# Local and pooled attention with a gated feed-forward: k and v in shared buffers, sums and half a softmax on other engines, an order chosen by replays

## Chip, cores and metric

The kernel runs on one core of one Trainium2 chip. The metric is device time of one execution in microseconds (us), lower is better; it is the median of several timed runs. Engines are named as the profile names them: PE (TensorE), PEld (its weight loads), DVE (VectorE), ACT (ScalarE), POOL (GpSimd), SP (the queue that issues most transfers).

## What is computed

Inputs are q, k and v of shape 8 x 8 x 576 x 64 (batch, heads, sequence, head dimension) and four weights. Cut to what matters:

```python
q_d, k_d, v_d = (mean of 4 neighbouring tokens of q, k, v)      # 144 rows
out_up  = repeat(softmax(q_d @ k_d.T / 8) @ v_d, 4)             # pooled attention
mask    = abs(i - j) < 4                                        # band: 7 keys for a query
out_loc = softmax(where(mask, q @ k.T / 8, -1e9)) @ v           # local attention
x = (out_up + out_loc) as 4608 tokens x 512
return ((x @ w1) * (x @ w2)) @ w3 @ w_out                       # 512 -> 1024 -> 1024 -> 512
```

All is float32; the large products run as three matmuls on high and low parts.

## The kernel before

Sequence and batch are cut into 24 units of 192 tokens (3 for each batch); two units make a chunk of 384 tokens, the piece that the feed-forward (`moe`) takes, so there are 12 chunks.

**Weights.** `fold` multiplies w3 and w_out into one matrix (tiles accw, then wphl); `gate_weights` makes high and low parts of w1 and w2. Each of the 40 pieces comes over DMA as 64-bit words (tile raw) and is turned into float32 by ACT or POOL (L293, L295), DVE (L298, L302) and ACT (L285).

**Pooled attention.** For each batch four `pair` calls make scores (s_ps), softmax (pexp: maximum on DVE L459, four exponentials on ACT L468, which also sum, scaling on POOL L477), transposes on PE (L484) and copies (pt). The values give oup. For batches 2 to 7 the sums over four tokens are made by accumulating DMAs that POOL issues (qks L410, vs L411).

**Local attention has two forms.** Batches 0 and 1 (units 0 to 5) are done in groups on PE (`group_unit`, `group_scores`, `group_values`): two quads a unit, 12 in all, each with scores of 128 x 432 elements in tile se. The mask is added (L627), then DVE takes the maximum (L636), subtracts it (L637), ACT takes the exponential (L638), DVE sums (L639), adds 1e-9, inverts (L640, L641) and scales (L642). PE transposes (te_ps) and multiplies by v.

Batches 2 to 7 (18 units) are done in `unit` on 128 partitions with 12 tokens each. For each of the seven offsets in the band, DVE multiplies q by the shifted k (tile pr, L727), and the product is summed over the head dimension by DVE (L740) or, for two offsets, by ACT in pieces with an accumulator (L737). After a softmax over seven values (tile s_t, L747 to L763), v times each weight is made by DVE (L794) or, for two offsets, by ACT (L786). Six additions sum the seven products into xl: the first and third by DVE (L804), the other four by an accumulating DMA from the tile pv into xl, which POOL issues (L802). DVE then turns the tile (L808), adds oup (L815), and the high and low parts go to chunk tiles xh and xl (ACT L821, DVE L822). The one buffer of k_t is loaded anew when the last product with it is done; v_t has two, pv three.

**Feed-forward.** For each chunk and each of eight f, PE makes two products (pab, 12 matmuls of 384 columns each), ACT copies the first (L870), DVE multiplies (tile a, L872), ACT and DVE make high and low parts (gh L877, gl L879), and PE accumulates into three banks (acc, 9 matmuls of 512 columns). Two sets of chunk tiles alternate.

**Order.** Each step is a task of a plan with an engine, a cost and what it depends on. `Plan.order` simulates the plan forwards and backwards 16 times with the costs as given and keeps the order with the least end. That order is fixed: each engine runs its own list from top to bottom, and a waiting instruction holds up all that stand behind it on its engine. PSUM has three banks for attention (ps), two for pab and three for acc.

Of the kernel before, what the change touches and what calls it, by code (L numbers as in the profile page):

```python
# [8 lines left out]
F32 = mybir.dt.float32  # L9
# [37 lines left out]
BUFS = dict(pr=3, pv=3, xl=2, xt=1, q=2, k=1, v=2, w3=5, early_raw=4, early_wx=2, late_raw=2, late_wx=2, a=2,  # L47
# [3 lines left out]
SHARE = dict(qk_pool=(), qk_act=(2, 4), av_act=(3, 5), dma_add=(2, 4, 5, 6))  # L51
# [3 lines left out]
ROUNDS = 16  # L55
# [24 lines left out]
class Plan:  # L80
# [29 lines left out]
    def run(self, prio, slack, back=False):  # L110
# [25 lines left out]
        while best:  # L136
            e = min(best, key=lambda e: best[e][0])
            s, i = best[e]
            t = tasks[i]
            x = s + t.cost  # L140
            free[e] = x
            again = {e}
            if t.late and back:
                dma = max(dma, s + 0.8) + t.late
                x = dma + 1.3 + t.cost
            elif t.late:
                dma = max(dma, x + 1.3) + t.late
                x = dma + 0.8
            start[i], end[i] = s, x
            order.append(i)  # L150
            ready[e].remove(i)
            for j in suc[i]:
                can[j] = max(can[j], x + (0.0 if e == tasks[j].eng == "PE" else LATENCY))
                left[j] -= 1
                if not left[j]:
                    ready[tasks[j].eng].append(j)
                    again.add(tasks[j].eng)
            for j in () if back else self.then[i]:
                can[j] = max(can[j], s)
                left[j] -= 1  # L160
                if not left[j]:
                    ready[tasks[j].eng].append(j)
                    again.add(tasks[j].eng)
            for e in sorted(again):
                if e in free:
                    choose(e)
        return max(end), start, end, order

    def order(self):

# [5 lines left out]
        now = self.run([-x for x in far], 0.05)  # L176
        best = now
        for _ in range(ROUNDS):
            back = self.run([-x for x in now[2]], 0.05, back=True)
            now = min((self.run([-x for x in back[2]], z) for z in SLACKS), key=lambda r: r[0])  # L180
            best = min(best, now, key=lambda r: r[0])
        self.best = best
        return [self.tasks[i] for i in best[3]]
# [26 lines left out]
def tile_attention_moe(ctx: ExitStack, tc: tile.TileContext, q, kw, vw, qk4, v4, w1, w2, w3, wout, edge, out):  # L210
# [234 lines left out]
    def pair(b, Q, P, lq, hq, hpt):  # L445
# [33 lines left out]
        for par in range(2):  # L479
            def flip(par=par):  # L480
# [4 lines left out]
            fl, bank = add("PE", 4 * 0.062, flip, [no], take=[R["ps"]], uses=[hp])  # L485

# [70 lines left out]
    def group_unit(n):  # L557
# [21 lines left out]
        def rest():  # L579
            hpt = None  # L580
            pts = []
            for qd, (U, hs, no) in enumerate(quads):
                for par in range(2):
                    def flip(par=par, U=U):
# [3 lines left out]
                    fl, bank = add("PE", NG * 0.062, flip, [no], take=[R["ps"]], uses=[hs])  # L588

# [9 lines left out]
                    pep.append(fl)  # L599
# [4 lines left out]
    def group_scores(b, j, qd, starts):  # L604
# [32 lines left out]
        t = add("DVE", dve_us(n2), lambda: nc.vector.tensor_tensor(out=p3(), in0=p3(), in1=wide_(U["mx"]), op=ALU.subtract), [t], uses=[hs])  # L637
        t = add("ACT", act_us(n2), lambda: nc.scalar.activation(out=U["p"], in_=U["p"], func=AF.Exp, scale=1.0 / D ** 0.5), [t], uses=[hs])  # L638
        t = add("DVE", dve_us(n2), lambda: nc.vector.tensor_reduce(out=U["sm"], in_=p3(), op=ALU.add, axis=AX.X), [t], uses=[hs])  # L639
        t = add("DVE", 0.16, lambda: nc.vector.tensor_scalar_add(U["sm"], U["sm"], 1e-9), [t], uses=[hs])  # L640
        t = add("DVE", 0.15, lambda: nc.vector.reciprocal(U["sm"], U["sm"]), [t], uses=[hs])  # L641
        no = add("DVE", dve_us(n2), lambda: nc.vector.tensor_tensor(out=p3(), in0=p3(), in1=wide_(U["sm"]), op=ALU.mult), [t], uses=[hs])  # L642
# [55 lines left out]
    def unit(n):  # L698
# [9 lines left out]
        def load_k():  # L708
            T["k"] = pools["dvp"].tile([128, nk], F32, name="k_t", bufs=BUFS["k"])
            nc.sync.dma_start(out=T["k"], in_=kw[b, :, j * nq:j * nq + nk])  # L710

        def load_v():
            T["v"] = pools["dvp"].tile([128, nk], F32, name="v_t", bufs=BUFS["v"])
            nc.sync.dma_start(out=T["v"], in_=vw[b, :, j * nq:j * nq + nk])
        lq, hq = add("SP", 0.5, load_q, take=[R["q"]], late=dma_us(128 * nq * 4))
        lk, hk = add("SP", 0.5, load_k, take=[R["k"]], late=dma_us(128 * nk * 4))
        lv, hv = add("SP", 0.5, load_v, take=[R["v"]], late=dma_us(128 * nk * 4))
# [55 lines left out]
        for i, o in enumerate(order):  # L773
# [26 lines left out]
            else:  # L800
                if i in share["dma_add"]:
                    t = add("Pool", 1.04, lambda o=o: nc.gpsimd.dma_start(out=T["x"], in_=T["pv", o], accum_op=ALU.add), [t, tm], uses=[hx, h], late=dma_us(128 * nq * 4, True))  # L802
                else:
# [23 lines left out]
    def moe(c):  # L827
# [56 lines left out]
        for i in range(3):  # L884
# [5 lines left out]
            def store(i=i):  # L890
                if c * CT // S in PB:
                    nc.sync.dma_start(out=out[c * CT + i * 128:c * CT + i * 128 + 128], in_=T["o", i])
                    return
                b, t = divmod(c * 2 * UT + i * 8, BT)
                if t + 8 <= BT:
                    nc.sync.dma_start(out=out_v[b, t:t + 8], in_=T["o", i])
                else:
                    r = BT - t
                    nc.sync.dma_start(out=out_v[b, t:], in_=T["o", i][:r * NB])
                    nc.sync.dma_start(out=out_v[b + 1, :8 - r], in_=T["o", i][r * NB:])  # L900
# [118 lines left out]
```

## Time and profile before

| | us |
|---|---|
| median of 3 timed runs | 819.2 |
| lowest and highest | 814.92, 820.14 |
| profiled execution | 811.43 |
| its span (first to last instruction) | 809.6 |
| PE, DVE, ACT, POOL busy in the span | 763.1, 645.4, 525.1, 200.3 |

The granted clock of PE was 0.987 over the span. Times in the trace count from the start of the span. The windows view gives each engine's busy time in a stretch; a busy time is the union of an engine's instructions. A row of a group gives count, busy time, mean length of one, and after the bar the idle time of the engine just before them with what ended it. A row of the waits view gives the sum of a wait, how often it came, and the longest. DVE starts an instruction some 0.08 us before the one ahead of it ends, so the starts of two long ones lie closer than one length.

### The profile page before, as it was taken

The numbers are of one execution on the slowest core, as the hardware profiler recorded it, in microseconds if no ns is written. First come the engines' busy times: TensorE is split into PE (matmuls) and PEld (weight loads), VectorE is DVE, ScalarE is ACT, GpSimd is POOL, SyncE is SP. The second block draws the span as 40 slices with busy tenths as digits, with TensorE's granted clock in tenths as the row PEclk, the third lists the DMA queues.
The fourth block names the chain that finished last, engine by engine and source line by source line (L and its number), as shares of the span: only waits on it lengthen the run. The fifth ranks groups of instructions, "written<-read, shape, count | busy, mean of one in ns | idle before, by whom it ended". The sixth has DMA issues, their size and how long they took to land.

```text
span 809.6 us, 15110 instructions
## 1 busy us (share of the span) xinstructions
PE 763.1 (94%) x5256; PEld 657.2 (81%) x5256; DVE 645.4 (80%) x1121; ACT 525.1 (65%) x2040; POOL 200.3 (25%) x211
## 2 busy tenths in 40 slices
PE   4899888999999999999999999999997999999995
PEld 1344467898999899998998999798997988999994
DVE  5889997967899998998999989799886898853111
ACT  4676656445877878867877697587783788742211
POOL 5321666300221323321312221222221221110000
PEclk9999999999999999999999999999998999999998
DMA  8975654813389759947858659855576853351101
GB/s 289 303 243 186 192 138 148 163 43 128 108 196 213 152 125 221 191 116 182 179 128 216 146 101 225 182 119 126 137 169 154 185 116 81 72 104 20 40 1 39
DMA packets 44067, 118.98 MB, mean 147 GB/s; under 512 B 5320, under 2 KB 11464, under 8 KB 43992
## 3 DMA queue, kind: packets, MB, share of 16 engines
q0 software_dynamic: 15264, 46.02, 32.5%
q1 hardware_dynamic: 28728, 72.01, 27.4%
q8 instruction: 41, 0.67, 0.3%
q14 instruction: 34, 0.28, 0.1%
HBM read 80.26 MB, written 9.44 MB: 111 GB/s over the span
## 4 chain that ended last, share of the span: by engine, by line
PE 59%; DVE 15%; DMA 14%; ACT 6%; issue 4%; POOL 0%; SPq 0%; DVEq 0%; ACTq 0%; POOLq 0%
PE pab L253 12%; PE pab L255 11%; PE pab L254 11%; PE acc L253 6%; PE acc L255 6%; PE acc L254 6%; DMA k_t<-in_kw_dram 4%; DMA xl<-pv 4%; DMA out_dram<-o_sb 3%; DVE pr L727 2%; DMA raw<-in_w_dram 2%; PE s_ps L456 2%; DVE wx L302 1%; ACT pexp L468 1%; DMA raw<-in_wout_dram 1%
## 5 line engine op out<-in xcount | busy, mean ns | idle before, releaser
L786 ACT ACTIVATE pv<-v_t,s_t 128x64 f32<-128x64 f32 x432 | 114.1, 343 | 28.3 <-DMA xl<-pv 16.1
L727 DVE TENSOR_TENSOR pr<-q_t,k_t 128x768 f32<-128x768 f32 x126 | 117.5, 951 | 15.7 <-DMA k_t<-in_kw_dram 15.7
L802 POOL DMA_DIRECT2D xl<-pv x72 | 65.2, 906 | 261.4 <-DVE xl L804 130.2
L737 ACT ACTIVATE junk<-pr 128x64 f32<-128x64 f32 x432 | 111.2, 257 | 19.7 <-DVE pr L727 9.5
L253 PE MATMUL acc<-wphl,gh 128*128 128x512 f32 x288 | 116.3, 404 | 1.7 <-ACT o_sb L887 1.7
L255 PE MATMUL acc<-wphl,gl 128*128 128x512 f32 x288 | 113.6, 395 | 1.8 <-DVE gl L879 1.8
L254 PE MATMUL acc<-wphl,gh 128*128 128x512 f32 x288 | 113.0, 392 | 0.0
L872 DVE TENSOR_TENSOR a<-pab,a 128x384 f32<-128x384 f32 x96 | 53.0, 552 | 55.4 <-PE pab L255 50.1
L870 ACT COPY a<-pab 128x384 f32<-128x384 f32 x96 | 45.7, 476 | 69.7 <-PE pab L255 55.2
L879 DVE TENSOR_TENSOR gl<-a,gh 128x384 fp32r<-128x384 f32 x96 | 55.7, 580 | 36.6 <-ACT gh L877 36.1
L740 DVE TENSOR_REDUCE s_t<-pr 128x12 f32<-128x768 f32 x90 | 84.0, 943 | 0.1
L737 ACT ACTIVATION_READ_ACCUMULATOR junk<-pr 128x1 f32 x432 | 81.7, 189 | 0.0
L877 ACT CAST gh<-a 128x384 fp32r<-128x384 f32 x96 | 49.0, 510 | 49.1 <-PE acc L254 39.5
L337 PE MATMUL accw<-wo,w 128*128 128x512 f32 x128 | 65.6, 646 | 15.7 <-DVE w L302 13.6
L477 POOL TENSOR_TENSOR pexp<-pexp,grs 72x576 f32<-72x576 f32 x32 | 50.4, 1576 | 111.1 <-DVE grs L476 63.5
L253 PE MATMUL pab<-xh,w2b 128*128 128x384 f32 x192 | 66.1, 344 | 5.0 <-DVE a L872 5.0
L794 DVE TENSOR_TENSOR pv<-v_t,s_t 128x768 f32<-128x768 f32 x72 | 70.5, 979 | 0.1
L253 PE MATMUL pab<-xh,w1b 128*128 128x384 f32 x192 | 66.4, 346 | 1.4 <-ACT a L870 1.4
L253 PE MATMUL pab<-xh,w1a 128*128 128x384 f32 x192 | 66.4, 346 | 0.5 <-DVE wphl L357 0.5
L253 PE MATMUL pab<-xh,w2a 128*128 128x384 f32 x192 | 66.2, 345 | 0.7 <-ACT a L870 0.7
L255 PEld LDWEIGHTS acc<-wphl,gl 128*128 128x128 f32 x288 | 54.2, 188 | 14.5 <-DVE gl L879 2.3
L255 PE MATMUL pab<-xh,w2b 128*128 128x384 f32 x192 | 65.4, 340 | 0.0
(109 smaller groups left out, 1832.2 us busy)
## 6 DMA issues: line engine op xcount, KB each, us to landing
xl<-pv POOLq DMA_DIRECT2D x72, 384.0 KB, 5.1
raw<-in_w_dram SPq DMA_DIRECT2D x32, 512.0 KB
qks<-in_qk_dram POOLq DMA_DIRECT2D x18, 576.0 KB, 7.9
k_t<-in_kw_dram SPq DMA_DIRECT2D x18, 576.0 KB
v_t<-in_vw_dram SPq DMA_DIRECT2D x18, 576.0 KB
out_dram<-o_sb SPq DMA_DIRECT2D x33, 256.0 KB
vs<-in_v_dram POOLq DMA_DIRECT2D x24, 288.0 KB, 5.8
q_t<-in_q_dram SPq DMA_DIRECT2D x18, 384.0 KB
```

The costliest lines, as they stand in the source:

```text
L253: nc.tensor.matmul(out_ps, lhsT=lh, rhs=rh, start=first, stop=False)
L254: nc.tensor.matmul(out_ps, lhsT=lh, rhs=rl, start=False, stop=False)
L255: nc.tensor.matmul(out_ps, lhsT=ll, rhs=rh, start=False, stop=last)
L337: nc.tensor.matmul(accs[m], lhsT=T["x"][:, j % 4 * 128:j % 4 * 128 + 128], rhs=wo[0][:, j], start=j == 0, stop=j == NF - 1)
L727: (nc.gpsimd if o in share["qk_pool"] else nc.vector).tensor_tensor(out=T[o], in0=T["q"], in1=T["k"][:, o * D:o * D + nq].rearrange("p (t ...
L737: nc.scalar.activation(out=junk, in_=T[o][:, t], func=AF.Copy, accum_out=T["s"][:, t, o:o + 1])
L740: reds.append(add("DVE", dve_us(nq), lambda o=o: nc.vector.tensor_reduce(out=T["s"][:, :, o], in_=T[o], op=ALU.add, axis=AX.X), [tp], uses ...
L786: nc.scalar.mul(out=T["pv", o][:, tt], in_=T["v"][:, (tt + o) * D:(tt + o + 1) * D], mul=T["s"][:, tt, o:o + 1])
L794: nc.vector.tensor_tensor(out=T["pv", o], in0=T["v"][:, o * D:o * D + nq].rearrange("p (t d) -> p t d", d=D), in1=T["s"][:, :, o].unsqueez ...
L802: t = add("Pool", 1.04, lambda o=o: nc.gpsimd.dma_start(out=T["x"], in_=T["pv", o], accum_op=ALU.add), [t, tm], uses=[hx, h], late=dma_us( ...
L872: tg = add("DVE", dve_us(CT), lambda f=f: nc.vector.tensor_tensor(out=T["a", f], in0=T["p", 1, f], in1=T["a", f], op=ALU.mult), [ta, ends[ ...
L879: tl = add("DVE", dve_us(CT), lambda f=f: nc.vector.tensor_tensor(out=T["gl", f], in0=T["a", f], in1=T["gh", f].bitcast(F32), op=ALU.subtr ...
```

## The change

**k and v share three buffers** (kv, taken in turn: k, v, k, v) in place of one for k and two for v.

**The four additions that were accumulating DMAs are tensor additions on POOL**, 128 x 768 each, 72 in all. `SHARE` has `dma_add=()` and `pool_add=(2, 4, 5, 6)`; the same additions of the chain are meant.

**Group softmax.** The subtraction, the sum and the scaling leave DVE. DVE scales the 128 x 6 maxima by -1/8; ACT runs six exponentials of 72 elements, each with its own bias and an accumulator that gives the sum; POOL scales by the inverse.

**Transposes in pairs.** The two transposing tasks of a `pair`, and of a quad in a group unit, are one task that takes two banks of three at once.

**Order.** Plans are made for four factors on transfer times, eight rounds each; each order found is replayed with four seeds in which durations vary, and the one with the lowest mean is kept.

**Stores** of the output are cut where a unit ends, so some are halves.

```diff
-BUFS = dict(..., k=1, v=2, ...)
+BUFS = dict(..., kv=3, ...)
-SHARE = dict(qk_pool=(), qk_act=(2, 4), av_act=(3, 5), dma_add=(2, 4, 5, 6))
+SHARE = dict(qk_pool=(), qk_act=(2, 4), av_act=(3, 5), dma_add=(), pool_add=(2, 4, 5, 6))
+SLOW = (1.0, 1.15, 1.3, 1.5)
+VARY = 0.04
+SEEDS = 4
-ROUNDS = 16
+ROUNDS = 8
...
+    def replay(self, order, seed):
+        rng, tasks = random.Random(seed), self.tasks
+        end, free, dma = [0.0] * len(tasks), {}, 0.0
+        for i in order:
+            t = tasks[i]
+            x = free.get(t.eng, 0.0)
+            for j in self.pre[i]:
+                x = max(x, end[j] + (0.0 if tasks[j].eng == t.eng == "PE" else LATENCY))
+            x += t.cost if t.eng in ("PE", "SP") else t.cost * (1 + abs(rng.gauss(0, VARY)))
+            free[t.eng] = x
+            if t.late:
+                dma = max(dma, x + 1.3) + t.late * (1.05 + abs(rng.gauss(0, 3 * VARY)))
+                x = dma + 0.8 + rng.random()
+            end[i] = x
+        return max(end)
...
-        for par in range(2):
-            def flip(par=par):
+        def flip():
+            for par in range(2):
                 T[par] = ps.tile([QB, 2, SD], F32, tag="g", name="t_ps", bufs=BUFS["ps"])
...
-            fl, bank = add("PE", 4 * 0.062, flip, [no], take=[R["ps"]], uses=[hp])
+        fl, *banks = add("PE", 8 * 0.062 + SWITCH / 2, flip, [no], take=[R["ps"], R["ps"]], uses=[hp])
...
-        t = add("DVE", dve_us(n2), lambda: nc.vector.tensor_tensor(out=p3(), in0=p3(), in1=wide_(U["mx"]), op=ALU.subtract), [t], uses=[hs])
-        t = add("ACT", act_us(n2), lambda: nc.scalar.activation(out=U["p"], in_=U["p"], func=AF.Exp, scale=1.0 / D ** 0.5), [t], uses=[hs])
-        t = add("DVE", dve_us(n2), lambda: nc.vector.tensor_reduce(out=U["sm"], in_=p3(), op=ALU.add, axis=AX.X), [t], uses=[hs])
+        t = add("DVE", 0.16, lambda: nc.vector.tensor_scalar_mul(U["mx"], U["mx"], -1.0 / D ** 0.5), [t], uses=[hs])
+        ex = []
+        for i in range(2 * NG):
+            ex.append(add("ACT", act_us(GK, 2), lambda i=i: nc.scalar.activation(out=p3()[:, i], in_=p3()[:, i], func=AF.Exp, bias=U["mx"][:, i:i + 1], scale=1.0 / D ** 0.5, accum_out=U["sm"][:, i:i + 1]), [t], uses=[hs]))
...
-        no = add("DVE", dve_us(n2), lambda: nc.vector.tensor_tensor(out=p3(), in0=p3(), in1=wide_(U["sm"]), op=ALU.mult), [t], uses=[hs])
+        no = [add("Pool", pool_us(n2), lambda: nc.gpsimd.tensor_tensor(out=p3(), in0=p3(), in1=wide_(U["sm"]), op=ALU.mult), [t], uses=[hs])]
...
-            T["k"] = pools["dvp"].tile([128, nk], F32, name="k_t", bufs=BUFS["k"])
+            T["k"] = pools["dvp"].tile([128, nk], F32, name="kv", bufs=BUFS["kv"])
...
                 if i in share["dma_add"]:
                     t = add("Pool", 1.04, lambda o=o: nc.gpsimd.dma_start(out=T["x"], in_=T["pv", o], accum_op=ALU.add), [t, tm], uses=[hx, h], late=dma_us(128 * nq * 4, True))
+                elif i in share["pool_add"]:
+                    t = add("Pool", pool_us(nq), lambda o=o: nc.gpsimd.tensor_tensor(out=T["x"], in0=T["x"], in1=T["pv", o], op=ALU.add), [t, tm], uses=[hx, h])
```

The order in three places. First POOL in the middle of the 18 units, where the four additions of one unit's xl stand; before, L802 is the accumulating DMA, L410 and L411 the pooled sums, L477 the scaling of a pair:

```order
L802 DMA xl_3923<-pv_3954 128x768
L410 DMA qks_3696<-in_qk4_dram 128x1152
L411 DMA vs_3855<-in_v4_dram 72x1024
L802 DMA xl_3923<-pv_4043 128x768
L411 DMA vs_3855<-in_v4_dram 72x1024
L802 DMA xl_3923<-pv_4098 128x768
L477 TENSOR_TENSOR pexp_4189<-pexp_4189,grs_4129 72x576
L802 DMA xl_3923<-pv_4222 128x768
L802 DMA xl_4249<-pv_4291 128x768
```

And now, with L831 the addition, L502 the scaling and L436 the pooled sum of v:

```order
L436 DMA vs_3238<-in_v4_dram 72x1024
L502 TENSOR_TENSOR pexp_3346<-pexp_3346,grs_3317 72x576
L436 DMA vs_3238<-in_v4_dram 72x1024
L831 TENSOR_TENSOR xl_3369<-xl_3369,pv_3387 128x768
L436 DMA vs_3238<-in_v4_dram 72x1024
L831 TENSOR_TENSOR xl_3369<-xl_3369,pv_3491 128x768
L831 TENSOR_TENSOR xl_3369<-xl_3369,pv_3505 128x768
L831 TENSOR_TENSOR xl_3369<-xl_3369,pv_3563 128x768
L502 TENSOR_TENSOR pexp_3570<-pexp_3570,grs_3530 72x576
```

Where four DMAs were issued with other issues between them, four additions stand, the last three in a row, ahead of the next pair's scaling.

Second DVE in the weights' stretch, at the softmax of the first quads (se, emx, esm); before, L298 and L302 are steps of the weights:

```order
L637 TENSOR_TENSOR se_599<-se_599,emx_600 128x432
L298 SCALAR_TENSOR_TENSOR raw_515<-raw_515 128x512
L636 TENSOR_REDUCE emx_622<-se_621 128x6
L639 TENSOR_REDUCE esm_601<-se_599 128x6
L637 TENSOR_TENSOR se_621<-se_621,emx_622 128x432
L302 SCALAR_TENSOR_TENSOR w3_641<-w3_641,raw_515 128x512
L627 TENSOR_TENSOR se_661<-se_ps_643,band_77 128x216
L640 TENSOR_SCALAR esm_601<-esm_601 128x6
L627 TENSOR_TENSOR se_661<-se_ps_644,band_77 128x216
L641 RECIPROCAL esm_601<-esm_601 128x6
L639 TENSOR_REDUCE esm_623<-se_621 128x6
L642 TENSOR_TENSOR se_599<-se_599,esm_601 128x432
```

And now, with L323 and L327 the steps of the weights and L663 the small scaling of the maxima:

```order
L662 TENSOR_REDUCE emx_587<-se_586 128x6
L323 SCALAR_TENSOR_TENSOR raw_489<-raw_489 128x512
L327 SCALAR_TENSOR_TENSOR w3_591<-w3_591,raw_489 128x512
L323 SCALAR_TENSOR_TENSOR raw_518<-raw_518 128x512
L663 TENSOR_SCALAR emx_587<-emx_587 128x6
L327 SCALAR_TENSOR_TENSOR w3_616<-w3_616,raw_518 128x512
L653 TENSOR_TENSOR se_629<-se_ps_598,band_77 128x216
L653 TENSOR_TENSOR se_629<-se_ps_599,band_77 128x216
L662 TENSOR_REDUCE emx_630<-se_629 128x6
L323 SCALAR_TENSOR_TENSOR raw_539<-raw_539 128x512
L663 TENSOR_SCALAR emx_630<-emx_630 128x6
L653 TENSOR_TENSOR se_662<-se_ps_637,band_77 128x216
```

Subtraction, sum and scaling of 432 elements are gone from the list, and weight steps stand closer together between what is left.

Third SP at the first loads of units 6 and 7; before, L710 loads k, L706 q, L714 v, L892 stores:

```order
L710 DMA k_t_2253<-in_kw_dram 128x1152
L706 DMA q_t_2263<-in_q_dram 128x768
L714 DMA v_t_2266<-in_vw_dram 128x1152
L706 DMA q_t_2272<-in_q_dram 128x768
L714 DMA v_t_2282<-in_vw_dram 128x1152
L892 DMA out_0_dram<-o_sb_2448 128x512
L710 DMA k_t_2467<-in_kw_dram 128x1152
L706 DMA q_t_2470<-in_q_dram 128x768
```

And now, with L737 for k, L741 for v, L733 for q and L927 for stores:

```order
L737 DMA kv_2311<-in_kw_dram 128x1152
L733 DMA q_t_2313<-in_q_dram 128x768
L733 DMA q_t_2323<-in_q_dram 128x768
L741 DMA kv_2325<-in_vw_dram 128x1152
L737 DMA kv_2330<-in_kw_dram 128x1152
L927 DMA out_0_dram<-o_sb_2423 128x512
L927 DMA out_0_dram<-o_sb_2457 64x512 x2
L927 DMA out_0_dram<-o_sb_2484 128x512
L733 DMA q_t_2531<-in_q_dram 128x768
L741 DMA kv_2535<-in_vw_dram 128x1152
L737 DMA kv_2829<-in_kw_dram 128x1152
```

The second k stood behind a store and waited for the only k buffer; now it stands ahead of the store, with a free third buffer.

67 lines of the change are left out of this document (37 added, 30 removed).

## The prediction

> **What bounds the kernel now.** I read the page's busy line first, then the windows, then who waited for whom in each of them, and last the rows of single instructions.
>
> ```profile
> PE 763.1 (94%) x5256; PEld 657.2 (81%) x5256; DVE 645.4 (80%) x1121; ACT 525.1 (65%) x2040; POOL 200.3 (25%) x211
> ```
>
> Windows cut at the places where the work changes (start, weights and group units, pipeline, the last chunks, output):
>
> ```profile
> core 0: us, PE busy (x) PEld busy (x) DVE busy (x) ACT busy (x) POOL busy (x), PEclk, DMA share, GB/s
> 0.00:20.00 20.00, 7.87 (x10) 2.51 (x11) 11.93 (x25) 9.93 (x14) 11.60 (x27) 1.00 0.89 288
> 20.00:160.00 140.00, 124.73 (x1223) 79.37 (x1222) 124.14 (x243) 88.73 (x210) 62.59 (x58) 0.99 0.69 196
> 160.00:715.00 555.00, 545.07 (x3585) 496.30 (x3584) 486.53 (x819) 407.31 (x1779) 123.52 (x123) 0.99 0.65 149
> 715.00:800.00 85.00, 85.00 (x442) 78.97 (x441) 22.76 (x36) 18.11 (x37) 2.59 (x3) 1.00 0.13 28
> 800.00:810.00 10.00, 0.46 (x3) 0.04 (x1) 0.00 (x0) 0.99 (x2) 0.00 (x0) 0.64 0.29 79
> ```
>
> PE is the bound, at full granted clock. It is idle 12.1 us in the first 20 us, 15.3 us from 20 to 160, 9.9 us from 160 to 715, never from 715 to 800, and about 9.5 us while the output leaves. The first and last of these the change doesn't touch: what can be won is 15.3 + 9.9 = 25.2 us, and a little that the modelled ends of matmuls hide. DVE is next: 124.1 of 140 us in the second window, 486.5 of 555 us (88%) in the third, so 68.5 us idle there. What PE waited for before 150 us, and then after it:
>
> ```profile
> PE accw L337 <- DVE w L302: 13.6, 5, 9.0
> PE t_ps L484 <- POOL pexp L477: 3.0, 3, 1.2
> PE te_ps L587 <- DVE esm L641: 2.0, 1, 2.0
> ```
> ```profile
> PE pab L253 <- DVE a L872: 5.0, 2, 4.5
> PE acc L255 <- DVE gl L879: 1.8, 1, 1.8
> PE acc L253 <- ACT o_sb L887: 1.7, 1, 1.7
> PE pab L253 <- ACT a L870: 1.4, 1, 1.4
> ```
>
> So PE's losses are mostly DVE being late. What DVE itself waited for longest between 150 and 715, the longest DMA in the chain that ended last, and ACT's wait on a transfer in the same stretch:
>
> ```profile
> DVE pr L727 <- DMA k_t<-in_kw_dram: 15.7, 6, 6.3
> ```
> ```profile
> 600.54 16.91 DMA k_t<-in_kw_dram
> ```
> ```profile
> ACT pv L786 <- DMA xl<-pv: 16.1, 8, 3.4
> ```
>
> The single k buffer is the largest cause: at 600 us a load of k, started only when the last product with the old k was done, kept DVE waiting 16.9 us of the chain, and the longest of the 5.0 us that PE waits for the product a lies in that stretch. ACT's 16.1 us are for pv buffers that an accumulating DMA still reads.
>
> **The group softmax and the start.** For each of 12 quads DVE loses the subtraction, the sum and the scaling, and gets one tiny scaling (nearest row L460); ACT trades one exponential for six with an accumulator.
>
> ```profile
> L637 DVE TENSOR_TENSOR se<-se,emx 128x432 f32<-128x432 f32 x12 | 9.4, 787 | 0.1
> L639 DVE TENSOR_REDUCE esm<-se 128x6 f32<-128x432 f32 x12 | 7.0, 590 | 0.4 <-ACT se L638 0.3
> L642 DVE TENSOR_TENSOR se<-se,esm 128x432 f32<-128x432 f32 x12 | 7.2, 603 | 0.1
> L638 ACT ACTIVATE se<-se 128x432 f32<-128x432 f32 x12 | 6.8, 566 | 8.4 <-DVE se L637 8.4
> L460 DVE TENSOR_SCALAR gnb<-gmx 72x4 f32<-72x4 f32 x32 | 5.8, 182 | 0.9
> L737 ACT ACTIVATE junk<-pr 128x64 f32<-128x64 f32 x432 | 111.2, 257 | 19.7 <-DVE pr L727 9.5
> L737 ACT ACTIVATION_READ_ACCUMULATOR junk<-pr 128x1 f32 x432 | 81.7, 189 | 0.0
> ```
>
> DVE: 9.4 + 7.0 + 7.2 - 12 x 0.18 = 21.4 us less. ACT: the nearest row is the 64-element sum, 0.257 + 0.189 = 0.45 us with its accumulator read, so 72 x 0.45 = 32 us come and 6.8 us go, 25 us more; ACT has 140 - 88.7 = 51 us free in that window, which covers it. Without that cover the exponentials would be the new start bound, and te_ps transposes late next. POOL gets 12 scalings, each about 1.1 us (by the fit below), and while one runs it can hold DVE up as the adds do: 12 x 0.27 = 3 us. DVE is thus some 18 us lighter where it is 89% busy and PE idles 15.3 us. PE can't get all of it: the accw waits of 13.6 us are for the weights, whose first part comes over DMA at 0.89 share, and the chain of one quad becomes longer (six short exponentials and a POOL step in a row). Ends: 0 (weights set the pace) and 15.3. I take half of 18: **-9 us**. Transposes in pairs issue the same 256 + 72 transposes; they need two of the three banks at once and so may start one copy later. I price that at nothing, because the pairs lie between chunk matmuls that PE can go on with, and at 3.0 us, what t_ps loses now, if that cover is gone.
>
> **Loads of k and v.** In the SP rows two k loads now stand before the first stores, and a k waits for the v of the unit before last and not for the products of its own forerunner. No DMA is added for it; the 15.7 us of DVE idle goes, unless stores ahead of it in SP's queue block. For PE this is worth the 5.0 us behind it and about 1 of the others: **-6 us**, between 0 and 9.9.
>
> **The adds.** 72 accumulating DMAs leave, 72 x 384 KB = 28.3 of the software queue's 46 MB, with 65 us of issuing on POOL; 72 tensor additions of 128x768 come. The trace has none on POOL; its nearest rows are an add of 288 and a subtraction of 512 elements, both from SBUF.
>
> ```profile
> L549 POOL TENSOR_TENSOR qks<-qks,k x8: 792/1192/1343, 12.8 to 90.9; 128x288 f32<-128x288 f32 x8
> L386 POOL TENSOR_TENSOR w1b<-wx,w1b x4: 1267/1270/1275, 115.3 to 128.8; 128x512 fp32r<-128x512 f32 x4
> q0 software_dynamic: 15264, 46.02, 32.5%
> xl<-pv POOLq DMA_DIRECT2D x72, 384.0 KB, 5.1
> L802 POOL DMA_DIRECT2D xl<-pv x72 | 65.2, 906 | 261.4 <-DVE xl L804 130.2 <-DMA xl<-pv 25.6 <-DVE pv L794 23.2
> ```
>
> By the shortest of each, (1.267 - 0.792)/224 = 2.12 ns an element, so 1.267 + 256 x 2.12 ns = **1.81 us**, against 5.1 us from issue to landing for the DMA. POOL has the time: 72 x 1.81 = 130 us in place of 65. The three last adds of a unit stand in a row on POOL; behind them wait pexp, and so t_ps on PE, by at most 3 x 1.81 = 5.4 us, which the pairs' lead over `up` covers.
>
> What POOL does to DVE is the larger term. A DVE instruction with two SBUF inputs that meets a POOL one runs late: timeline of POOL, then of DVE.
>
> ```profile
> 283.60 1.14 POOL L477 TENSOR_TENSOR pexp<-pexp,grs 72x576 f32<-72x576 f32 x1 [2.60 <-ACT junk L737]
> ```
> ```profile
> 283.35 0.92 DVE L740 TENSOR_REDUCE s_t<-pr 128x12 f32<-128x768 f32 x1
> 284.18 1.38 DVE L794 TENSOR_TENSOR pv<-v_t,s_t 128x768 f32<-128x768 f32 x1
> ```
>
> The reduction (one input) keeps its length; the product begins at 284.18, ends at 285.56, and 0.95 before that is 284.61, near POOL's end at 284.74: it waited. How much this costs on average, by the groups:
>
> ```profile
> L727 DVE TENSOR_TENSOR pr<-q_t,k_t 128x768 f32<-128x768 f32 x126 | 117.5, 951 | 15.7 <-DMA k_t<-in_kw_dram 15.7
> L794 DVE TENSOR_TENSOR pv<-v_t,s_t 128x768 f32<-128x768 f32 x72 | 70.5, 979 | 0.1
> L804 DVE TENSOR_TENSOR xl<-xl,pv 128x768 f32<-128x768 f32 x36 | 35.5, 987 | 2.4 <-ACT pexp L468 1.0 <-DMA xl<-pv 0.9 <-ACT pv L786 0.5
> L879 DVE TENSOR_TENSOR gl<-a,gh 128x384 fp32r<-128x384 f32 x96 | 55.7, 580 | 36.6 <-ACT gh L877 36.1
> L872 DVE TENSOR_TENSOR a<-pab,a 128x384 f32<-128x384 f32 x96 | 53.0, 552 | 55.4 <-PE pab L255 50.1
> L815 DVE TENSOR_TENSOR xt<-xt,oup 128x768 f32<-128x768 f32 x18 | 17.1, 949 | 0.1
> L477 POOL TENSOR_TENSOR pexp<-pexp,grs 72x576 f32<-72x576 f32 x32 | 50.4, 1576 | 111.1 <-DVE grs L476 63.5
> ```
>
> Over the plain lengths (951 for 768 elements, 552 for 384, where L872 reads PSUM and never waits) the excess is 72 x 28 + 36 x 36 + 96 x 28 ns = 6.0 us, and some 0.5 us on tiny ones. The six batches of 4 pairs after 160 us run 24 scalings of 1.14 us: 0.27 us of DVE stall each. That is the lower end for an add. An add holds 0.67 us longer, so 0.27 + 0.67 = 0.94 if every longer hold met a two-input instruction. These are 117.5 + 70.5 + 35.5 + 55.7 and three groups like L815 at 17 us, 330 of 486 us, 68%; so 0.27 + 0.67 x 0.68 = 0.73 us, and 72 x 0.73 = 52 us. DVE would be busy 486.5 + 52 = 538.5 of 555 us. Can it? In one stretch of the trace
>
> ```profile
> 240.00:280.00 40.00, 40.00 (x255) 36.98 (x254) 38.20 (x60) 32.16 (x150) 11.20 (x11) 1.00 0.84 175
> ```
>
> DVE is 95.5% busy and PE loses nothing. At that share 538.5 us need 564: **+9 us**. The ends: 0.27 gives 506 us of work, 530 us long, no loss; 0.94 gives 554, 580 us long, +25.
>
> **Order chosen for varying durations, split stores.** The order moves no work between engines. Stores are cut at units, 48 in place of 39; the nine more issues stand on SP, which waits most of the time for what it stores or loads into, so nothing; without that cover they would delay loads of k and v, which now stand further ahead. The profiled execution took 811.4 us (span 809.6 and 1.8 around it), the timed runs 814.9 to 820.1; with the accumulating DMAs gone from the waits I let half of the 7.8 us between it and the median stay, 3.9.
>
> Sum: 811.4 - 9 - 6 + 9 = 805.4 as the profiled execution would be; + 3.9 = **809 us**, 1.2% under the median of 819.2. About 1%, 8.2 us, is what a measurement of this kernel can tell from no change.
>
> **Rivals.** *The port decides (slower).* Each add stops DVE longer than I take, POOL's three adds in a row above all, and DVE becomes the bound of the 18 units. The Trainium skill ("SBUF — State Buffer", Who interferes with whom) has one exclusive lock between GpSimd and a VectorE instruction with two SBUF inputs, held for the whole instruction; by that rule the trace's late product is no accident. Worked out from rows: a stall of the whole 1.81 us for the 68% is 1.23 us, 89 us in all, 575 us of DVE work, 602 long: +47, so 847; at 0.94 it is 825. I price it at 836. It decides from 0.6 us an add, where 555 x 0.955 - 486.5 = 43.5 us are used up. For it: DVE's 88%. Against: scalings often ran while DVE reduced or waited, and then cost nothing.
>
> *The order carries (faster still).* Stalls stay at 0.27, and most of the 25.2 us of PE idle goes: -20, 791, with 3.9 then 795. Against: half of it hangs on weights.
>
> *Nothing seen.* PE is the bound, the start follows the weights, the k waits were hidden but for 5 us, and the stalls take it back: 818. This is also the case in which adds on POOL merely replace DMAs that nobody waited for.
>
> **How the numbers follow.** Forecast, 803 to 815, 0.40; the order carries 0.19; nothing seen 0.20; the port decides 0.21. Of the forecast 0.25 lies under 811.0. Faster by over 1%: 0.19 + 0.25 = 0.44; within: 0.15 + 0.20 = 0.35; slower: 0.21. The range runs from 792, short of the order's 795, to 836, the port's middle.
>
> **What would show it.** Right: POOL's adds near 1.81 us when alone; the means of pr, pv and gl above 951 and 552 by enough to make some 52 us; DVE near 538 us of the third window with PE's idle there still about 10; no wait on k; PE's idle from 20 to 160 near 6 us; software queue 18 MB. Wrong: PE waiting for a or gl in many places after 200 us (the port), or PE's idle from 20 to 160 us still near 15 (the start).

## Result and the profile after

| | before | changed |
|---|---|---|
| median, us | 817.06 | 878.06 |
| lowest to highest, us | 814.78 to 820.14 | 872.12 to 880.1 |
| profiled execution, us | 811.43 | 879.14 |

The changed kernel takes 1.073 of the time (95% interval 1.066 to 1.080): 61 us slower, where 809 was forecast and the range ended at 836. (The median of before is of four runs here, of three in the table further up.) The execution of before that was traced is 5.6 us under its median, so the two traces lie further apart, 67.7 us, than the medians. The busy line of the page first:

```profile
PE 792.5 (90%) x5256; PEld 669.3 (76%) x5256; DVE 724.7 (83%) x1097; ACT 543.1 (62%) x2172; POOL 317.6 (36%) x223
```

DVE has 24 instructions fewer than before and is busy 79.3 us longer. The windows are cut as those of before were, the pipeline's now ending near 780 us (columns: the stretch, its length, busy time of PE, PEld, DVE, ACT and POOL with counts, granted clock, DMA share, GB/s):

```profile
20.00:160.00 140.00, 125.79 (x1128) 80.38 (x1127) 111.61 (x220) 99.87 (x300) 68.81 (x64) 0.98 0.67 191
160.00:780.00 620.00, 575.47 (x3703) 510.05 (x3703) 561.50 (x806) 409.91 (x1799) 221.72 (x125) 0.96 0.36 91
780.00:866.00 86.00, 81.96 (x416) 75.29 (x415) 38.62 (x47) 21.69 (x56) 15.60 (x7) 0.98 0.04 11
```

In the start DVE is 12.5 us lighter and PE does what it did (125.8 us against 124.7). Nearly all of the loss is in the 18 units: the stage is some 65 us longer, and PE idles 44.5 us there, where it idled 9.9. The rest is mostly that PE is busy longer with the same work: over the whole span its 5256 instructions take 792.5 us, before 763.1. The granted clock was 0.965 over the span (0.96 in this stage) and 0.987 before (0.99). In e4 below, which has this order without the stalls, PE is busy 762.1 us at 0.992, so the longer busy time comes and goes with the stalls; what lowered the clock was not tried apart. What PE waited for, longest first:

```profile
PE pab L278 <- DVE a L901: 26.1, 18, 5.0
PE pab L278 <- ACT a L899: 17.5, 9, 4.2
PE accw L362 <- DVE w L327: 9.9, 4, 9.0
PE accw L362 <- DVE wo L327: 6.4, 4, 3.0
PE acc L280 <- DVE gl L908: 4.8, 5, 1.8
```

The waits for a and gl, 5.0, 1.4 and 1.8 us before, are now 48 us in 32 places. ACT's part leads to DVE as well:

```profile
ACT a L899 <- DVE gl L908: 46.0, 22, 5.6
```

The groups of DVE (count, busy time, mean ns of one):

```profile
L754 DVE TENSOR_TENSOR pr<-q_t,kv 128x768 f32<-128x768 f32 x126 | 153.4, 1235 | 0.4 <-ACT junk L764 0.3
L821 DVE TENSOR_TENSOR pv<-kv,s_t 128x768 f32<-128x768 f32 x72 | 88.0, 1227 | 0.7 <-POOL xl L831 0.4
L767 DVE TENSOR_REDUCE s_t<-pr 128x12 f32<-128x768 f32 x90 | 83.8, 942 | 0.1
L908 DVE TENSOR_TENSOR gl<-a,gh 128x384 fp32r<-128x384 f32 x96 | 70.5, 734 | 29.9 <-ACT gh L906 29.6
L901 DVE TENSOR_TENSOR a<-pab,a 128x384 f32<-128x384 f32 x96 | 52.7, 549 | 51.5 <-PE pab L280 49.9 <-ACT junk L764 0.7 <-ACT a L899 0.5
L500 DVE TENSOR_SCALAR grs<-gsm 72x4 f32<-72x4 f32 x32 | 12.4, 387 | 2.9 <-ACT pexp L493 2.7
L788 DVE TENSOR_SCALAR sm<-sm 128x12 f32<-128x12 f32 x18 | 8.6, 477 | 0.6
```

The means of DVE's instructions with two SBUF inputs lie 29 to 33% over their plain lengths, which are those without POOL beside them (pr 1235 and pv 1227 against 951; gl 734 against 552). What reads one tile (the reduction, 942) or one tile and PSUM (a, 549) did not grow, but tiny scalings did. Their lengths before:

```profile
L475 DVE TENSOR_SCALAR grs<-gsm 72x4 f32<-72x4 f32 x32 | 5.3, 165 | 5.9 <-ACT pexp L468 5.7
L761 DVE TENSOR_SCALAR sm<-sm 128x12 f32<-128x12 f32 x18 | 3.5, 192 | 0.6
```

Over the plain lengths the sum is 126 x 284 + 72 x 276 + 96 x 182 ns = 73.1 us for pr, pv and gl, 5.7 us for the other additions of 768, and 24.3 us for tiny ones (the scalings grs 7.1, sm 5.1 and gnb 3.6, and 8.5 for two steps of the softmax with two inputs of 84 elements): 103 us, less the 6.5 us that the same sum gave before, 97 us, or **1.34 us for each of 72 adds**. DVE's busy time agrees within 4 us: 97 less the 21.4 us that left DVE with the group softmax is 75.6, and it grew by 79.3.

POOL's adds, the shortest, median and longest in ns, and their mean:

```profile
L831 POOL TENSOR_TENSOR xl<-xl,pv x72: 1807/2424/4232, 228.9 to 802.4; 128x768 f32<-128x768 f32 x72
```
```profile
L831 POOL TENSOR_TENSOR xl<-xl,pv 128x768 f32<-128x768 f32 x72 | 164.2, 2280 | 196.4 <-DVE xl L833 176.5 <-DVE pv L821 18.2
```

An add takes 1.81 us alone, as worked out, and 2.28 on average: POOL waits for DVE as DVE does for POOL. One place shows how. The timeline of DVE and of POOL (start, length):

```profile
394.97 1.73 DVE L833 TENSOR_TENSOR xl<-xl,pv 128x768 f32<-128x768 f32 x1
396.62 0.95 DVE L851 TENSOR_TENSOR xl<-xt,xh 128x768 fp32r<-128x768 f32 x1
397.49 2.58 DVE L754 TENSOR_TENSOR pr<-q_t,kv 128x768 f32<-128x768 f32 x1
400.00 2.58 DVE L821 TENSOR_TENSOR pv<-kv,s_t 128x768 f32<-128x768 f32 x1
402.50 0.94 DVE L767 TENSOR_REDUCE s_t<-pr 128x12 f32<-128x768 f32 x1
403.36 2.89 DVE L754 TENSOR_TENSOR pr<-q_t,kv 128x768 f32<-128x768 f32 x2
406.18 0.55 DVE L908 TENSOR_TENSOR gl<-a,gh 128x384 fp32r<-128x384 f32 x1
```
```profile
396.77 4.99 POOL L831 TENSOR_TENSOR xl<-xl,pv 128x768 f32<-128x768 f32 x2 [0.89 <-DVE xl L833]
402.72 1.85 POOL L831 TENSOR_TENSOR xl<-xl,pv 128x768 f32<-128x768 f32 x1 [0.96 <-DVE pv L821]
```

The addition that ends at 396.70 releases POOL, which has two adds in a row. The first waits until L851 is over (397.57), then takes 1.8 us; pr, begun at 397.49, waits all of them and takes 2.58 instead of 0.95. The second add waits for pr (400.07), and pv for the add: the engines take turns. The reduction beside the third add keeps 0.94; the next pr loses 1.0. Behind them stood gl, whose operand ACT had ready near 402.6, and behind gl ACT's copy of a, and PE:

```profile
406.76 0.48 ACT L899 COPY a<-pab 128x384 f32<-128x384 f32 x1 [3.54 <-DVE gl L908]
```
```profile
407.29 0.44 PE L278 MATMUL pab<-xh,w1b 128*128 128x384 f32 x1 [2.37 <-ACT a L899]
```

### The profile page after: what moved, and what is told of

Read it like the earlier page. It is cut to its first block, busy times and chain, and to the rows that moved or that the text cites. A ratio compares the mean times of both kernels' runs of the same rounds, so it can differ in the third digit from the quotient of the medians.

```text
span 877.4 us, 15181 instructions
## 1 busy us (share of the span) xinstructions
PE 792.5 (90%) x5256; PEld 669.3 (76%) x5256; DVE 724.7 (83%) x1097; ACT 543.1 (62%) x2172; POOL 317.6 (36%) x223
## 4 chain that ended last, share of the span: by engine, by line
PE 46%; DVE 36%; ACT 8%; issue 7%; DMA 2%; POOL 0%; SPq 0%; DVEq 0%; ACTq 0%; POOLq 0%
PE pab L278 9%; PE pab L279 8%; PE pab L280 8%; DVE pr L754 7%; DVE pv L821 5%; PE acc L278 4%; PE acc L280 4%; PE acc L279 4%; PE accw L362 4%; DVE gl L908 3%; DVE s_t L767 3%; DVE xl L833 2%; DVE a L901 2%; ACT pv L813 2%; ACT pexp L493 2%
## 5 line engine op out<-in xcount | busy, mean ns | idle before, releaser
L831 POOL TENSOR_TENSOR xl<-xl,pv 128x768 f32<-128x768 f32 x72 | 164.2, 2280 | 196.4 <-DVE xl L833 176.5
L754 DVE TENSOR_TENSOR pr<-q_t,kv 128x768 f32<-128x768 f32 x126 | 153.4, 1235 | 0.4 <-ACT junk L764 0.3
L813 ACT ACTIVATE pv<-kv,s_t 128x64 f32<-128x64 f32 x432 | 113.0, 340 | 15.4 <-DVE s_t L790 11.1
L278 PE MATMUL acc<-wphl,gh 128*128 128x512 f32 x288 | 118.7, 412 | 0.0
L279 PE MATMUL acc<-wphl,gh 128*128 128x512 f32 x288 | 114.5, 397 | 0.0
L502 POOL TENSOR_TENSOR pexp<-pexp,grs 72x576 f32<-72x576 f32 x32 | 54.6, 1706 | 162.7 <-DVE grs L501 88.0
L908 DVE TENSOR_TENSOR gl<-a,gh 128x384 fp32r<-128x384 f32 x96 | 70.5, 734 | 29.9 <-ACT gh L906 29.6
L821 DVE TENSOR_TENSOR pv<-kv,s_t 128x768 f32<-128x768 f32 x72 | 88.0, 1227 | 0.7 <-POOL xl L831 0.4
L278 PE MATMUL pab<-xh,w2b 128*128 128x384 f32 x192 | 69.5, 362 | 18.7 <-DVE a L901 18.7
L278 PE MATMUL pab<-xh,w1b 128*128 128x384 f32 x192 | 68.5, 357 | 9.3 <-ACT a L899 9.1
L279 PE MATMUL pab<-xl,w1a 128*128 128x384 f32 x192 | 65.7, 342 | 2.0 <-DVE xl L702 2.0
```

The source lines that it names most:

```text
L278: nc.tensor.matmul(out_ps, lhsT=lh, rhs=rh, start=first, stop=False)
L279: nc.tensor.matmul(out_ps, lhsT=lh, rhs=rl, start=False, stop=False)
L754: (nc.gpsimd if o in share["qk_pool"] else nc.vector).tensor_tensor(out=T[o], in0=T["q"], in1=T["k"][:, o * D:o * D + nq].rearrange("p (t ...
L813: nc.scalar.mul(out=T["pv", o][:, tt], in_=T["v"][:, (tt + o) * D:(tt + o + 1) * D], mul=T["s"][:, tt, o:o + 1])
L821: nc.vector.tensor_tensor(out=T["pv", o], in0=T["v"][:, o * D:o * D + nq].rearrange("p (t d) -> p t d", d=D), in1=T["s"][:, :, o].unsqueez ...
L831: t = add("Pool", pool_us(nq), lambda o=o: nc.gpsimd.tensor_tensor(out=T["x"], in0=T["x"], in1=T["pv", o], op=ALU.add), [t, tm], uses=[hx, h])
```

## Experiments

Theories: P, POOL's adds shut DVE's two-input instructions out; O, the other parts (order, buffers, softmax) lose the time; L, POOL itself is late. The medians of before in the shared runs were 817.34 (e1 to e4), 816.29 (e5 to e8) and 814.87 (e9 to e12). A kernel with one part alone is planned anew, so it has an order of its own, and a difference of a few us can come from that; e4, e7 and e10 keep the changed kernel's order. Behind each median stands its ratio to before with the 95% interval; e4 and e10 rest on two runs each. The transposes in pairs and the split stores have no run of their own.

**e1: everything but the adds.**

```diff
-SHARE = dict(..., dma_add=(), pool_add=(2, 4, 5, 6))
+SHARE = dict(..., dma_add=(2, 4, 5, 6), pool_add=())
```

> The changed kernel with the four additions of each unit back on accumulating DMAs; everything else of the change stays (shared buffers, group softmax, pairs, replayed order, made anew for these costs). Theory P (POOL's additions lock DVE's two-input instructions out, some 97 us of DVE time): 805 to 825 us, and the means of pr and pv back to about 0.95 us. Theory O (the new order, the shared buffers or the softmax lose the time, the additions little): still over 860 us. Theory L (not the lock: POOL itself is late, what waits for POOL is late behind it): 805 to 825 too.

822.37 us, 1.007 (1.004 to 1.010): the adds hold nearly all of the loss, and the rest with DMA adds is no gain. Its products take their plain length, and POOL's queue now stands behind landings (the idle time ahead of its additions, DMA part 25.6 before). PE's longest wait after the weights is for the scaling of a pair (pexp), which stands in that queue:

```profile
L754 DVE TENSOR_TENSOR pr<-q_t,kv 128x768 f32<-128x768 f32 x126 | 117.0, 949 | 1.3 <-DMA q_t<-in_q_dram 1.2
L829 POOL DMA_DIRECT2D xl<-pv x72 | 62.5, 867 | 272.5 <-DVE xl L833 123.7 <-DMA xl<-pv 72.5 <-DVE pv L821 16.9
```
```profile
PE t_ps L510 <- POOL pexp L502: 11.6, 2, 6.3
```

**e2: the kernel before with POOL adds alone.**

```diff
-SHARE = dict(..., dma_add=(2, 4, 5, 6))
+SHARE = dict(..., dma_add=(), pool_add=(2, 4, 5, 6))
...
+                elif i in share["pool_add"]:
+                    t = add("Pool", pool_us(nq), lambda o=o: nc.gpsimd.tensor_tensor(out=T["x"], in0=T["x"], in1=T["pv", o], op=ALU.add), [t, tm], uses=[hx, h])
```

> The kernel before with this one part of the change: the four additions on POOL, the old search for the order. P and L: 865 to 890 us, the whole loss from one part. O: 815 to 830 us.

874.18 us, 1.068 (1.064 to 1.073). The one part costs nearly the whole time without the others, which speaks against O.

```profile
L727 DVE TENSOR_TENSOR pr<-q_t,k_t 128x768 f32<-128x768 f32 x126 | 133.9, 1079 | 4.4 <-DMA q_t<-in_q_dram 3.4 <-DMA k_t<-in_kw_dram 0.9
L794 DVE TENSOR_TENSOR pv<-v_t,s_t 128x768 f32<-128x768 f32 x72 | 93.2, 1298 | 0.1
```

**e3: the adds on DVE.**

```diff
-SHARE = dict(..., dma_add=(), pool_add=(2, 4, 5, 6))
+SHARE = dict(..., dma_add=(), pool_add=())
```

> The changed kernel with the four additions on DVE itself, so 72 x 0.87 = 63 us more of its own work and no POOL additions. P: DVE work is 486 + 63 = 549 us against 486 + 97, so 830 to 855 us, faster than the change as it stands although DVE does the work. O: 860 us or more. L: 830 to 855 us.

832.42 us, 1.019 (1.014 to 1.023). DVE did all 72 itself, 108 adds at 973 ns, and the kernel was still 46 us faster than with POOL's help: doing an add costs DVE 0.97 us, being shut out by one 1.34. (The 46 us are not the adds alone: this order has a slower start, with a granted clock of 0.88 from 20 to 160 us, where the changed kernel had 0.98.)

```profile
L833 DVE TENSOR_TENSOR xl<-xl,pv 128x768 f32<-128x768 f32 x108 | 105.1, 973 | 0.7 <-ACT pv L813 0.5
```

**e4: POOL writes and does not read.** Each add becomes two and a half fills of the same tile, so xl lacks four of its seven products; buffers, order and the waits on xl stay.

```diff
+        def fill(x):
+            for _ in range(2):
+                nc.gpsimd.memset(x, 0.0)
+            nc.gpsimd.memset(x[:, :UT // 2], 0.0)
...
-                    t = add("Pool", pool_us(nq), lambda o=o: nc.gpsimd.tensor_tensor(...), [t, tm], uses=[hx, h])
+                    t = add("Pool", pool_us(nq), lambda o=o: fill(T["x"]), [t, tm], uses=[hx, h])
```

> The changed kernel, its order and waits as they are, with each POOL addition replaced by POOL writing zeros to the same tile xl three times (full, full, half; an estimate of 1.9 us by the memset rows), so it leaves the sum of four of the seven products out. POOL is as long busy and in the same place of the chain but reads nothing. P: 800 to 825 us, pr and pv at 0.95 us. L and O: 865 us or more, since POOL is as late as before.

801.77 us, 0.980 (0.975 to 0.985).

```profile
160.00:715.00 555.00, 554.80 (x3750) 504.76 (x3749) 487.03 (x819) 416.76 (x1819) 201.88 (x265) 1.00 0.40 102
```
```profile
L754 DVE TENSOR_TENSOR pr<-q_t,kv 128x768 f32<-128x768 f32 x126 | 118.8, 961 | 0.5 <-ACT junk L764 0.3
```
```profile
L803 POOL MEMSET xl<- 128x768 f32 x144 | 107.6, 747 | 155.5 <-DVE xl L838 149.3
L804 POOL MEMSET xl<- 128x384 f32 x72 | 30.2, 419 | 4.1
```

POOL is as long at each place (2 x 0.747 + 0.419 = 1.91 us), DVE's products are plain, and PE idles 0.2 us in 555. So neither POOL's own time (L) nor the order (O) loses anything; the shutting out costs 878.1 - 801.8 = **76 us**, with the lower clock that comes with it. One more thing differs: a fill doesn't read pv, so POOL doesn't wait for pv (18.2 us in the changed kernel), and pv comes free without POOL. But what DVE and ACT waited for POOL's adds there is 2.7 us in all, too little for 76. What is left of the change, with neither DMA nor reads for these sums, is worth 15.6 us (817.3 - 801.8). The Trainium skill ("SBUF — State Buffer", Who interferes with whom) says that a VectorE instruction with two SBUF inputs meets a GpSimd one that reads SBUF, not one that only writes it: this run against the changed kernel agrees (961 ns for a product beside fills, 1235 beside adds).

**e10: POOL reads one tile** (two scalings of xl in place of an add; the same products are left out).

```diff
+        def fill(x):
+            for _ in range(2):
+                nc.gpsimd.tensor_scalar(out=x, in0=x, scalar1=1.0, scalar2=0.0, op0=ALU.mult, op1=ALU.add)
...
-                    t = add("Pool", pool_us(nq), lambda o=o: nc.gpsimd.tensor_tensor(...), [t, tm], uses=[hx, h])
+                    t = add("Pool", pool_us(nq), lambda o=o: fill(T["x"]), [t, tm], uses=[hx, h])
```

> The changed kernel, its order as it is, with each POOL addition replaced by two POOL instructions that read the tile xl alone and write it back times one (an estimate of 1.9 us for both), so it leaves the sum of four of the seven products out. If any POOL instruction that reads SBUF locks DVE's two-input instructions out: 860 us or more, pr near 1.2 us. If only POOL instructions with two inputs do: 800 to 810 us, pr at 0.95 us.

835.35 us, 1.025 (1.019 to 1.030), between e4 and the changed kernel and in neither of the two ranges.

```profile
L803 POOL TENSOR_SCALAR xl<-xl 128x768 f32<-128x768 f32 x144 | 186.0, 1292 | 151.5 <-DVE xl L837 142.7
```
```profile
L754 DVE TENSOR_TENSOR pr<-q_t,kv 128x768 f32<-128x768 f32 x126 | 135.7, 1095 | 0.4 <-ACT junk L764 0.3
L825 DVE TENSOR_TENSOR pv<-kv,s_t 128x768 f32<-128x768 f32 x72 | 80.6, 1124 | 0.0
```

Reading one tile is enough to stop DVE, but it stops it less (some 56 us by the sum above, where adds make 103). Whether that is because two short holds leave a gap between them, or because one tile is read and not two, this run can't tell.

**e7: each add in four pieces** of 192 elements.

```diff
+        def pieces(x, y):
+            for a in range(0, UT, 3):
+                nc.gpsimd.tensor_tensor(out=x[:, a:a + 3], in0=x[:, a:a + 3], in1=y[:, a:a + 3], op=ALU.add)
...
-                    t = add("Pool", pool_us(nq), lambda o=o: nc.gpsimd.tensor_tensor(...), [t, tm], uses=[hx, h])
+                    t = add("Pool", pool_us(nq), lambda o=o: pieces(T["x"], T["pv", o]), [t, tm], uses=[hx, h])
```

> The changed kernel with each POOL addition cut into four of 192 elements (an estimate of 0.6 us each from the rows of 288, 512 and 768 elements), order as it is. If what a DVE instruction loses is the rest of the POOL instruction it meets, and POOL seldom gets in again: stalls fall below 0.7 us an addition, 830 to 850 us. If POOL gets in again between any two DVE instructions, the sum of holds counts (4 x 0.6 = 2.4 us against 1.81): 875 to 900 us.

855.03 us, 1.051 (1.045 to 1.057): 23 us back, and between the two ranges.

```profile
L803 POOL TENSOR_TENSOR xl<-xl,pv 128x192 f32<-128x192 f32 x288 | 255.0, 925 | 138.4 <-DVE xl L837 132.0 <-DVE mx L779 5.0 <-DVE pv L825 1.4
```
```profile
L754 DVE TENSOR_TENSOR pr<-q_t,kv 128x768 f32<-128x768 f32 x126 | 134.3, 1084 | 0.4 <-ACT junk L764 0.3
```

DVE waits less, and POOL more: four pieces take 4 x 0.925 = 3.7 us on average where a whole add took 2.28, so the chain of xl grows. POOL doesn't wait at every piece: half of them take at most 0.61 us, near the shortest of 0.58 (the row stands in the last section), and the others, up to 2.8 us, make the mean.

**e11: two adds on POOL, two as DMAs.**

```diff
-SHARE = dict(..., dma_add=(), pool_add=(2, 4, 5, 6))
+SHARE = dict(..., dma_add=(5, 6), pool_add=(2, 4))
```

> The changed kernel with two additions of each unit on POOL and two on accumulating DMAs, order made anew. If the loss goes by the number of POOL additions, half of the way from 822 to 878: 840 to 858 us. If there is a point from which DVE decides and half stays under it, as the prediction has it (0.6 us an addition over 72, so 43.5 us of stalls; 36 additions give 36 x 1.35 = 49 us): 822 to 835 us.

821.66 us, 1.007 (1.003 to 1.011), as far above before as e1, though DVE now pays for 36 adds: some 35 us on pr, pv and gl over their plain lengths. The equal time doesn't show that they cost PE nothing, since the two orders differ. PE's wait for pexp falls from 11.6 us in e1 to 2.1, its wait for DVE's product a grows from 2.0 to 7.9, and the granted clock from 20 to 160 us is 0.92 in place of 0.96:

```profile
L754 DVE TENSOR_TENSOR pr<-q_t,kv 128x768 f32<-128x768 f32 x126 | 128.0, 1031 | 1.1 <-DMA kv<-in_kw_dram 1.0
L821 DVE TENSOR_TENSOR pv<-kv,s_t 128x768 f32<-128x768 f32 x72 | 84.5, 1179 | 2.2 <-POOL xl L831 1.7
```

```profile
PE pab L278 <- DVE a L901: 7.9, 10, 2.0
```

So most of these stalls don't reach PE, and in kind that is the slack of which the prediction speaks. How much of them does is not shown.

**e5: shared k and v alone.**

```diff
-BUFS = dict(..., k=1, v=2, ...)
+BUFS = dict(..., kv=3, ...)
```

> The kernel before with one part of the change: k and v in three shared buffers; the order is searched anew by the old search. If DVE's 15.7 us of waiting on k cost PE some 6 us, as the prediction has it: 807 to 813 us and no DVE wait on k over 3 us. If those waits were hidden: 815 to 820 us.

821.21 us, 1.007 (1.003 to 1.010): no gain, and above both ranges. DVE still waits for loads as long as before (15.7):

```profile
DVE pr L727 <- DMA kv<-in_kw_dram: 16.1, 6, 6.6
```

**e6: the group softmax alone.**

```diff
-        t = add("DVE", dve_us(n2), lambda: nc.vector.tensor_tensor(..., in1=wide_(U["mx"]), op=ALU.subtract), ...)
...
-        t = add("DVE", dve_us(n2), lambda: nc.vector.tensor_reduce(out=U["sm"], ...), ...)
...
+        for i in range(2 * NG):
+            ex.append(add("ACT", act_us(GK, 2), lambda i=i: nc.scalar.activation(..., accum_out=U["sm"][:, i:i + 1]), ...))
...
```

> The kernel before with the new group softmax alone (six exponentials on ACT, scaling on POOL), order searched anew by the old search. The prediction's step: DVE some 18 us lighter from 20 to 160 us, PE gets half, 806 to 811 us. Rival (the stretch from 20 to 160 us is set by the chain of the weights and by longer quads, not by DVE's load): 815 to 822 us, DVE busy in that stretch lower by 10 us or more and PE's idle there still about 15.

816.19 us, 1.002 (0.999 to 1.005). DVE is 10.3 us lighter in the start and PE only 0.4 us more busy; its wait for the weights is nearly as long as before (13.6):

```profile
20.00:160.00 140.00, 125.17 (x1112) 78.85 (x1111) 113.83 (x216) 97.18 (x291) 67.66 (x65) 0.95 0.69 193
```
```profile
PE accw L337 <- DVE w L302: 12.8, 5, 8.8
```

**e8: the choice of order alone** (SLOW, VARY, SEEDS, eight rounds, the replays).

```diff
...
+                found += [(sum(self.replay(r[3], k) for k in range(SEEDS)) / SEEDS, len(found) + i, r) for i, r in enumerate(tried)]
+        self.best = min(found, key=lambda f: f[:2])[2]
-        self.best = best
-        return [self.tasks[i] for i in best[3]]
```

> The kernel before with the new choice of order alone (four factors on transfers, replays with varying durations). If that choice helps where accumulating DMAs vary: 800 to 812 us. If it does nothing that can be told: 813 to 821 us. If the order itself is part of the 5 us that the change with DMA additions lost: 822 us or more.

833.38 us, 1.025 (1.019 to 1.030): beside accumulating DMAs the new choice loses.

```profile
PE t_ps L509 <- POOL pexp L502: 11.0, 5, 3.6
PE acc L280 <- DVE gl L904: 8.4, 1, 8.4
```
```profile
L827 POOL DMA_DIRECT2D xl<-pv x72 | 63.5, 886 | 295.7 <-DVE xl L829 147.8 <-DMA xl<-pv 74.6 <-DVE pv L819 35.5
```

POOL's queue stands 75 us behind landings (26 before), pexp stands in that queue, and PE waits for pexp. Why the replays prefer such an order was not tried.

**e9: the last two DMA adds to DVE**, in the kernel before.

```diff
-SHARE = dict(..., dma_add=(2, 4, 5, 6))
+SHARE = dict(..., dma_add=(2, 4))
```

> The kernel before with two of the four accumulating DMAs of each unit (the two that end the chain) as additions on DVE, order searched anew by the old search. DVE gets 36 x 0.87 = 31 us more of its own work, which its 68 us of idle can take, and the chain of a unit loses two landings of 5.1 us. If the adds belong on neither POOL nor all on DVE: 808 to 816 us. If DVE has in truth no room: 820 to 830 us.

**807.72 us**, 0.991 (0.988 to 0.994): 0.9% under the kernel before. The interval leaves out 1, but the 7 us are a little less than the 8.2 that the prediction takes to be telling, and it is one order.

```profile
160.00:715.00 555.00, 550.28 (x3722) 500.77 (x3722) 508.48 (x861) 406.00 (x1766) 107.28 (x90) 1.00 0.53 125
```
```profile
L804 DVE TENSOR_TENSOR xl<-xl,pv 128x768 f32<-128x768 f32 x72 | 71.3, 992 | 7.9 <-DMA xl<-pv 7.9
```

DVE takes 36 adds (22 us more busy, 92%) and PE idles 4.7 us in place of 9.9.

**e12: the scaling of a pair on ACT**, in the kernel before.

```diff
-        no = add("Pool", pool_us(4 * SD), lambda: nc.gpsimd.tensor_tensor(...), [rs], uses=[hg, hp])
+        for i in range(4):
...
+                nc.scalar.mul(out=p[:, i], in_=p[:, i], mul=T["rs"].rearrange("p a c -> p (a c)")[:, i:i + 1])
...
```

> The kernel before with the scaling of each pair on ACT (four instructions of 144 elements) in place of POOL, order searched anew: no two-input POOL instruction is left after the weights. DVE loses its 6.5 us of stalls there, ACT gets some 40 us more, and the scaling no longer stands behind accumulating DMAs in POOL's queue. If that is worth something to PE: 806 to 813 us. If PE's bound hides it: 814 to 820 us. If ACT becomes late: over 822 us.

821.07 us, 1.006 (1.004 to 1.009), although DVE is busy 12 us less from 160 to 715. So taking POOL's scalings from beside DVE brought nothing there; why it is slower stays open.

## Why the prediction was wrong

**The step that failed is the sum of the adds:** "0.27 + 0.67 x 0.68 = 0.73 us, and 72 x 0.73 = 52 us". Measured are 1.34 us an add and 97 us. By the prediction's own rule 486.5 + 97 = 583.5 us of work at 95.5% take 611, +56 in place of +9. In the sum that gives 856 in place of 809; 9 more are the start's (below), and the last 13 up to 878 stay open. The sum has no term for the granted clock, which fell with the stalls. Three things were wrong in that step.

- *The sample.* 0.27 came from 24 scalings, released one by one, many while DVE reduced or waited; and that their row has a mean of 1.58 us against 1.14 for one alone says that it was often POOL that waited. The adds are released by DVE's own adds and products, stand in a row, and meet a stretch in which DVE goes from one two-input instruction to the next; the timeline shows a stall of 1.6 us, 1.6 and 1.0 for three adds. The upper bound of 0.94 rested on the same sample and bounded nothing.
- *The victims.* Tiny instructions make 24 of the 103 us, 15.8 of them scalings that read one tile. The prediction had put the tiny ones at 0.5 us in the kernel before and gave them no share in the sum for the adds.
- *The slack.* DVE was to run at 95.5% before PE loses. It ran at 90.6% (561.5 of 620) with PE idle 44.5 us. From e4 to e10 DVE's stalls grow by some 48 us (56 less the 8 that e4 still has) and the time by 33.6; from e10 to the changed kernel by 47 us, and the time by 42.7. (The two groups of runs differ by 2.5 us in the kernel before.) By this rough count, in which the lower clock is part of the times, some 15 us were taken up for nothing, not the 43.5 of "It decides from 0.6 us an add". A stretch of 40 us without loss does not say that a stage can hold its share.

**The rivals.** The port decides had the right mechanism and sign and too small a price (836). Even its harshest sum, a stall of 1.23 us and a time of 847, lies under the 1.34 and 878 that came. The other two fail.

**The start, -9: about 0.** "I take half of 18" was wrong, its end at 0 was right: e6 takes DVE's load away and gains nothing, and the changed kernel's PE is busy 1.1 us more from 20 to 160 and idle 14.2 us, where about 6 was said to show that the prediction is right.

**Loads, -6: the wait went, but not by the buffers.** The shared buffers alone leave the wait on k (e5). In e1, e4 and the changed kernel it is gone, but it is gone in e8 and e9 too (at most 0.9 us), which keep one buffer for k and have only another order or fewer DMAs. Nor is it shown to be worth 6 us: e1 is no faster than before. With e4, PE's idle from 160 to 715 falls from 9.9 to 0.2 us, past the 6, and with e9 to 4.7. Only these two runs get below 9.9, and both have fewer accumulating DMAs; e3, with none into xl but a busier DVE, idles 18.1. Which of the DMAs delayed what was not tried apart.

**The gap of 3.9 us to the median** is not seen: the changed kernel's profiled execution lies 1.1 us above its median, e4's 0.7 below. The execution of before from which the term came was a low one of its kernel, whose runs spread from 809.6 to 821.9.

**What held:** 1.81 us for an add alone, the DMA adds gone from the software queue

```profile
q0 software_dynamic: 4896, 17.70, 12.3%
```

(18 MB said), and the sign for wrong that was named: PE waiting for a or gl in many places after 200 us.

## What to carry to other kernels

Before work moves to POOL, ask what DVE runs beside it: an add that POOL does can cost a busy DVE more (1.34 us here) than doing it itself (0.97). Price it by what DVE does in the very stretch that releases it, not by a mean over instructions released elsewhere. An accumulating DMA cost POOL's queue and transfers, but left DVE's products at their plain length (949 ns in e1). A split between DMAs and the engine with slack (e9) was 0.9% faster than all four as DMAs; all four on DVE were tried only with the rest of the change (e3, 832 us).

## What the runs showed of the hardware

POOL work of about one length (1.65 to 1.91 us for a place, when alone) does different things to DVE: beside fills that only write, a product takes 961 ns on average, beside two scalings that read one tile 1095, beside an add that reads two 1235. The waiting goes both ways: POOL's adds take 2.28 us on average for 1.81 alone, and each of four pieces 0.93 on average where the shortest took 0.58:

```profile
L803 POOL TENSOR_TENSOR xl<-xl,pv x288: 582/608/2784, 230.9 to 784.4; 128x192 f32<-128x192 f32 x144
```

Unexpected was that DVE's scalings of 4 and 12 elements wait as well (165 to 387 ns, 192 to 477), while a reduction of 768 (942) and a reciprocal of 4 (173 to 172) do not.
